# Attention, expert layer and a second layer in one kernel: float64 loads issued three jobs ahead, weight splits begun one step later

## The chip, the core and the metric

The kernel runs on one core of a Trainium2 chip. The core has a matrix engine (TensorE, PE in the rows), a vector engine (VectorE, DVE), a scalar engine (ScalarE, ACT), GpSimd (POOL) and SyncE (SP), which here only issues DMA transfers, all on one queue. Each engine takes its own instructions in order and waits for the others by semaphores. The metric is the device time of the whole program in microseconds, the median over several runs.

## The reference

```python
def _attn_ref(q, k, v, alpha):          # 2 batches, 8 heads, 768 tokens, 48 features, float32
    for t in range(S):
        state = alpha[:, :, t, :, None] * state + np.einsum('bhd,bhe->bhde', k[:, :, t], v[:, :, t])
        y[:, :, t] = np.einsum('bhd,bhde->bhe', q[:, :, t], state)

def _moe_ref(x, w_gate, w1, w2, capacity):      # 1536 tokens of 384, 8 experts of 1024, float32
    expert_idx = np.argmax(x @ w_gate, axis=1)  # each token goes to one expert, scaled by its gate
    h = np.maximum(np.einsum('ecd,edf->ecf', disp, w1), 0.0)
    y = np.einsum('ecf,efd->ecd', h, w2)

def _moe2_ref(x, w_in, w_out):          # 384 -> 2048 -> 384, both weights float64
    h = x @ w_in
    sp = np.where(h > 20.0, h, np.log1p(np.exp(np.minimum(h, 20.0))))
    return ((h * np.tanh(sp)) @ w_out).astype(np.float32)
```

## The kernel before

The program has three stages. In the **attention stage** (to about 80 us) the tokens go in 12 tiles of 128. Routing is part of it: each tile's rows are scattered by GpSimd (`scatter`, L108) into a table `tab` in DRAM, ordered by expert. Filler products (`keep_busy`, L783), whose results nobody reads, stand at the very start and in some gaps of TensorE.

The **expert stage** walks 8 experts with 8 steps each, 64 steps in all. At a step `g1` (L1052, nine matmuls) makes 128 hidden features for 240 tokens; ScalarE's ReLU writes `hh` (L1056) and VectorE the rest `hl` (L1057). `g2` (L1069, nine matmuls) of the step three before follows. Every product is made of three with operands split into a high and a low part. The result of `g1` goes to one of two PSUM banks in turn, so `g1` of step s waits until `hl` of step s−2 has been read out. Behind step 5 of an expert, `xpose` turns the next expert's tokens, gathered from `tab` (`gather`, L124), on TensorE.

The weights of w1 and w2 come in pieces of 128 x 768, two for each two steps: a DMA into a buffer `st` (L324; 8 buffers in `erl`, 6 in `wst`), the high part by ScalarE (`whi`, L336), the low part by VectorE (`wlo`, L342). `conv_to(n)` splits all pieces below n; `load_to` keeps the loads a fixed number of pieces ahead (`AHEAD`, 13). Step s calls `conv_to` with its bound behind its products.

Beside that the float64 weights `w_in` and `w_out` are made float32 in 17 jobs spread over steps 3 to 60 by the table `job_at`: `cvt_load` (L222, 512 KB into one of three buffers `big`), `cvt_a` (two ScalarE rows, L195 and L230, and two VectorE rows, L198 and L201) and `cvt_b` (one VectorE row, L206, and a store to DRAM, L238). Job 0 has its `cvt_a` at step 3 and its `cvt_b` at step 4, job 1 at 6 and 7, job 2 at 9 and 11, job 3 at 12 and 15, job 4 at 16 and 17. Behind `cvt_b(n)` the load of job n+2 is issued. The converted weights come back as pieces for the **last stage** (from 214 us), which is the second layer: `f1` (L1132), the activation, `f2` (L1175) and a scatter of the output rows.

Small works stand at fixed steps: `check_all` (whether the decay's inverse is good, L775 to L778) at step 0, `places` and `sort_places` at steps 1 and 2.

The order on every engine is that of the code (a manual schedule); waits follow from tiles that share a buffer. SP also waits with each transfer for the one issued eight before.

Of the kernel before, what the change touches and what calls it, by code (L numbers as in the profile page):

```python
# [23 lines left out]
def kernel(  # L24
# [41 lines left out]
    ATT = 4  # L66
# [4 lines left out]
    LEAD = 6  # L71
    WST = 6
# [11 lines left out]
    def w_new(i):  # L84
        p = wr_p[2 if i >= 76 else (i + 8) % 12 < 8]
        whi[i], wlo[i] = (p.tile([128, PW], F32R, tag=t, name=f"{t}{i}") for t in ("whi", "wlo"))
# [44 lines left out]
    bk = [ps.tile([128, 512], F32, name=f"bk{i}") for i in range(8)]  # L131
# [84 lines left out]
    def words(t):  # L216
        return t.bitcast(U32).rearrange("p (f two) -> p f two", two=2)

    def cvt_load(n):
        if n < len(cvt_jobs):  # L220
            t = words(fpool[0].tile([128, 2 * CN], F32, tag="big", name="w64", bufs=3)[:, 0:2 * cvt_jobs[n][1].shape[1]])
            nc.sync.dma_start(out=t, in_=words(cvt_jobs[n][0]))  # L222
            cvt_t[n] = [t]
# [35 lines left out]
    def late_load(n):  # L259
        if not 0 <= n < NLATE:  # L260
            return
        st = wst.tile([128, PW], F32, tag="st", name=f"sd{n}")
        fs = slice(FH + n // 2 * 128, FH + (n // 2 + 1) * 128)
        if n % 2:
            nc.sync.dma_start(out=words(st), in_=words(w_out[fs, :]))
        else:
            nc.sync.dma_start(
                out=st.bitcast(U32).rearrange("p (k f) -> p k f", k=KD),
                in_=w_in.bitcast(U32)[:, 2 * fs.start:2 * fs.stop].rearrange("(k p) f -> p k f", p=128),
            )  # L270
        late_t[n] = st
# [39 lines left out]
            hi, lo, w = late_t.pop(n)[3:]  # L311
            nc.vector.tensor_tensor(out=lo, in0=w, in1=hi.bitcast(F32), op=ALU.subtract)

    AHEAD = WST + 7
    conv_n, load_n, cvt_n = [0], [0], [0]

    def written(i):
        return min((i - E * NP1) // 4 * 6 + 6, len(cvt_jobs)) if i >= E * NP1 else 0

    def load_to(n):  # L320
        while load_n[0] < min(n, len(pieces)) and cvt_n[0] >= written(load_n[0]):
            i = load_n[0]
            st = raw_p[i % 14 >= 8].tile([128, PW], F32, tag="st", name=f"st{i}")
            nc.sync.dma_start(out=st.rearrange("p (a b) -> p a b", b=pieces[i].shape[2]), in_=pieces[i])  # L324
            wst_t[i] = st
            load_n[0] += 1
# [3 lines left out]
    def conv_high(n):  # L330
        while conv_n[0] < min(n, len(pieces)):
            i = conv_n[0]
            load_to(i + 1 + AHEAD)
            w = wst_t.pop(i)
            w_new(i)
            nc.scalar.activation(out=whi[i], in_=w, func=AF.Copy)  # L336
            low.append((i, w))
            conv_n[0] += 1

    def conv_low(n=None):  # L340
        for i, w in low[:n]:
            nc.vector.tensor_tensor(out=wlo[i], in0=w, in1=whi[i].bitcast(F32), op=ALU.subtract)  # L342
        del low[:n]

    def conv_to(n):
        conv_high(n)
        conv_low()
# [10 lines left out]
    with ExitStack() as actx:  # L358
# [414 lines left out]
        def check_all(cm):  # L773
            cmt = misc[0:1, 0:128]
            nc.tensor.transpose(out=cmt, in_=cm, identity=ident)  # L775
            cmx = const.tile([1, 1], F32, name="cmx")
            nc.vector.tensor_reduce(out=cmx, in_=cmt, axis=AX.X, op=ALU.min)
            nc.vector.tensor_scalar(out=bad, in0=cmx, scalar1=1.0, scalar2=None, op0=ALU.is_lt)  # L778


        def keep_busy(t, n):
            for _ in range(n):
                nc.tensor.matmul(out=t, lhsT=busy[:, 0:128], rhs=busy, start=True, stop=True)  # L783
# [56 lines left out]
                    )  # L840


        keep_busy(bk[6], 12)
        for h in range(2):
            load_an(0, range(h * HP // 2, (h + 1) * HP // 2))
        load(qn_t, 0, q_t, "qn")
# [138 lines left out]
        i = NTILE - 1  # L985
# [28 lines left out]
    x2l = x2p.tile([128, KD, XW], F32R, name="x2l")  # L1014
    fp = main.enter_context(tc.tile_pool(name="fp", bufs=2))
    fpool[0] = fp

    def big_tile():
        return fp.tile([128, 1024], F32, tag="big", name="big", bufs=3)
# [25 lines left out]
    def g1(e, m):  # L1045
        xh, xl = xt_e[e]
        wh, wl = w_first(e, m)
        hps = bk[2 + m % 2][:, m // 2 % 2 * WB:m // 2 % 2 * WB + WIN]
        n = 0
        for a, b_ in ((wh, xh), (wl, xh), (wh, xl)):  # L1050
            for kk in range(KD):
                nc.tensor.matmul(out=hps, lhsT=a[:, kk], rhs=b_[:, kk, :], start=(n == 0), stop=(n == 3 * KD - 1))  # L1052
                n += 1
        hh = fp.tile([128, WIN], F32R, tag="hh", name="hh", bufs=LAG + 1)
        hl = fp.tile([128, WIN], F32R, tag="hl", name="hl", bufs=LAG + 1)
        nc.scalar.activation(out=hh, in_=hps, func=AF.Relu)  # L1056
        nc.vector.scalar_tensor_tensor(  # L1057
            out=hl, in0=hps, scalar=0.0, in1=hh.bitcast(F32), op0=ALU.max, op1=ALU.subtract
        )
        h_t[e, m] = (hh, hl)  # L1060
# [27 lines left out]
    def y_out(e):  # L1088
        y_put(4 + e % 2 * 2, off_v.pop(e), free=e == E - 1)
# [4 lines left out]
    def place(col, engines=DYN):  # L1094
        return nc.values_load(meta_i[0:1, col:col + 1], engines=engines, min_val=0, max_val=NT)


    def places():
        nc.vector.tensor_tensor_scan(out=inc, data0=tot, data1=zn[:, 0:E], initial=0.0, op0=ALU.add, op1=ALU.add)
        nc.vector.tensor_tensor(out=off, in0=inc, in1=tot, op=ALU.subtract)  # L1100
        nc.vector.tensor_copy(out=meta_i, in_=off)


        nc.vector.scalar_tensor_tensor(
            out=slow_f, in0=mxc[0:1], scalar=float(WIN), in1=bad, op0=ALU.is_gt, op1=ALU.max
        )
# [113 lines left out]
    def at(n):  # L1220
        return steps[n] if 0 <= n < NS else None


    def f_mish(n):
        late = (n - EARLY) // 2 if n > EARLY else -9
        if n % 2 == 0:
            late_high(late - 1)
            sigma(at(n)) if at(n) else None
            late_size(late)
        elif at(n):  # L1230
            sigma(at(n))
        if n in last_of:
            bs = [at(i) for i in last_of[n]]
            cosine(bs)
        for m, c in full:
            (f_out if m >= MA else f_keep)(c)
        full.clear()
        now = list(due)
        due.clear()
        if n in last_of:  # L1240
            due.extend(bs)
        for b in now:
            gated(b)
        if n % 2:
            late_low(late - 2)
            late_join(late - 1)
            late_load(late + LATE_AHEAD - 1)
        conv_to(E * MF - EARLY + n + 3 + LEAD)

    def f_head(n):  # L1250
        if at(n):
            f1(at(n))
        f_mish(n)
# [28 lines left out]
        part(last, cs[3], True)  # L1282

    EARLY = LAG2
    CVT_END = 45
    LATE_AHEAD = 3
    xpose(0, False)
# [8 lines left out]
    for n in range(2 * len(cvt_jobs)):  # L1296
        job_at.setdefault(free[n * CVT_END // (2 * len(cvt_jobs))], []).append(((cvt_a, cvt_b)[n % 2], n // 2))
    for e in range(E):
        for m in range(MF):
            step = e * MF + m  # L1300
            if m == 6:
                off_v[e] = place(e)
            g1(e, m)
            pend.append((e, m))
            if len(pend) > LAG:
                pe, pm = pend.pop(0)
                g2(pe, pm)
                if pm == MF - 1:
                    y_out(pe)
            if e == E - 1 and m >= MF - EARLY:  # L1310
                f_head(m - MF + EARLY)
            conv_to(min(step + 1 + LEAD, ATT + (step + 1) * 9 // 8))
            if step == 0:
                cvt_load(0)
                cvt_load(1)
            for f, n in job_at.get(step, ()):
                f(n)
                if f is cvt_b:
                    cvt_load(n + 2)
            if step == 0:  # L1320
                check_all(cm)
            if step == 1:
                places()
            if step == 2:
                sort_places()
            if step % 4 == 3 and 0 < step // 4 <= NTILE:
                tok_scatter(step // 4 - 1)
            if e == E - 1 and m == 0:
                nc.sync.dma_start(
                    out=srt, in_=toks.rearrange("(c p) o -> p (c o)", p=128), allow_slow_non_contiguous=True  # L1330
                )
            if step == E * MF - 4:
                cvt_marks()
            if step == E * MF - 2:
                cvt_flag()
            if m == 5 and e + 1 < E:
                xpose(e + 1)
                if e + 2 < E:
                    gather(e + 2)
    for pe, pm in pend:  # L1340
        g2(pe, pm)
    apart.append(at(EARLY))
    f1(at(EARLY))
    y_out(E - 1)
# [240 lines left out]
```

## Time and profile before

| | |
|---|---|
| time, median of 3 runs | 433.04 us (432.83 to 433.56) |
| the profiled execution | 433.29 us, of it 431.0 us span from the first to the last instruction |
| TensorE busy | 413.6 us (96%) |
| VectorE busy | 325.6 us (76%) |
| ScalarE busy | 327.5 us (76%) |
| DMA | 68.89 MB, mean 160 GB/s |

Times in the rows below are counted from the start of the span. TensorE's busy time is modelled from pipelined matmuls, so idle time on it is the safer reading; the stages' limits differ, and the shares above are means over all of them.

### The profile page before, as it was taken

What the parts mean: (1) busy time and instruction counts of PE and PEld (TensorE: products, weight loads), DVE (VectorE), ACT (ScalarE), POOL (GpSimd) and SP (SyncE); (2) the same over time, 40 slices, a digit from 0 to 9 for tenths busy, and PEclk for the clock granted to TensorE, in tenths of its full rate; (3) what the DMA queues carried; (4) which work ended last, traced back from release to release, by engine and by line L of the source; (5) the groups of instructions that cost most, each with busy time, mean ns of one, the idle gap of its engine ahead of it and who ended that gap; (6) DMA issues with size and microseconds to landing.
All of it is one profiled execution on the core that took longest, in us unless ns stands there. A gap on an engine that the chain in (4) does not pass through costs nothing.

```text
span 431.0 us, 8400 instructions
## 1 busy us (share of the span) xinstructions
PE 413.6 (96%) x3122; PEld 376.7 (87%) x3126; DVE 325.6 (76%) x647; ACT 327.5 (76%) x579; POOL 61.4 (14%) x76
## 2 busy tenths in 40 slices
PE   7999989989999999999999999999999999999994
PEld 3887877789899999999988898989899898889893
DVE  7999997779799899988837875976697456475551
ACT  5887996668688787877779788878887877797630
POOL 5122666212011012000000000000000000003033
PEclk9899999999999999999999999999999999999999
DMA  7999996499999999995170112111000000001022
GB/s 226 331 299 320 321 364 236 149 318 247 364 334 328 321 287 314 297 337 189 40 238 0 39 36 74 38 37 53 23 1 2 0 2 0 2 1 73 2 75 78
DMA packets 51565, 68.89 MB, mean 160 GB/s; under 512 B 5500, under 2 KB 41852, under 8 KB 51516
## 3 DMA queue, kind: packets, MB, share of 16 engines
q1 hardware_dynamic: 49596, 63.55, 47.7%
q0 software_dynamic: 1920, 4.73, 3.0%
q8 instruction: 26, 0.43, 0.4%
q14 instruction: 23, 0.19, 0.2%
HBM read 56.65 MB, written 11.61 MB: 158 GB/s over the span
## 4 chain that ended last, share of the span: by engine, by line
PE 76%; DVE 9%; DMA 6%; ACT 4%; issue 2%; SPq 1%; POOL 0%; ACTq 0%; POOLq 0%; DVEq 0%
PE bk L1175 23%; PE bk L1132 22%; PE bk L1052 12%; PE bk L1069 11%; DMA w<-in_w_out_dram 2%; DVE pt L457 2%; PE bk L519 2%; DMA an<-in_alpha_t_dram 1%; DMA w<-in_w_in_dram 1%; PE bk L565 1%; DMA xs<-tab 1%; ACT whi L336 1%; PE bk L583 1%; PE bk L554 1%; PE bk L783 1%
## 5 line engine op out<-in xcount | busy, mean ns | idle before, releaser
L342 DVE TENSOR_TENSOR wlo<-st,whi 128x768 fp32r<-128x768 f32 x74 | 69.9, 951 | 16.1 <-ACT whi L336 15.2
L1160 DVE TENSOR_TENSOR p<-p,bk 128x512 f32<-128x512 f32 x48 | 32.8, 683 | 51.4 <-ACT p L1150 51.4
L1175 PE MATMUL bk<-whi,big 128*128 128x384 f32 x240 | 66.7, 338 | 0.8 <-DVE x2l L1079 0.8
L336 ACT ACTIVATE whi<-st 128x768 fp32r<-128x768 f32 x74 | 61.7, 842 | 0.0
L1144 ACT ACTIVATE p<-bk 128x512 f32<-128x512 f32 x48 | 28.8, 599 | 35.0 <-PE bk L1132 33.5
L1069 PE MATMUL bk<-hl,whi 128*128 128x240 f32 x192 | 52.8, 275 | 0.0
L1069 PE MATMUL bk<-hh,wlo 128*128 128x240 f32 x192 | 52.7, 274 | 0.0
L1069 PE MATMUL bk<-hh,whi 128*128 128x240 f32 x192 | 52.6, 274 | 0.0
L1175 PEld LDWEIGHTS bk<-whi,big 128*128 128x128 f32 x240 | 44.1, 188 | 2.6 <-DVE x2l L1079 1.1
L108 POOL DMA_INDIRECT out_dram<-acc,srt x12 | 12.2, 1018 | 233.9 <-DVE acc L1199 229.8
L1132 PE MATMUL bk<-x2l,whi 128*128 128x512 f32 x144 | 41.7, 397 | 0.0
L1132 PE MATMUL bk<-x2h,wlo 128*128 128x512 f32 x144 | 41.1, 394 | 0.0
L1132 PE MATMUL bk<-x2h,whi 128*128 128x512 f32 x144 | 41.0, 393 | 0.0
L1175 PE MATMUL bk<-wlo,big 128*128 128x384 f32 x120 | 40.6, 338 | 0.0
L1056 ACT ACTIVATE hh<-bk 128x240 fp32r<-128x240 f32 x64 | 23.5, 367 | 20.5 <-PE bk L1052 19.2
L1052 PE MATMUL bk<-xh,whi 128*128 128x240 f32 x192 | 33.6, 283 | 3.1 <-DVE hl L1057 2.7
L1069 PEld LDWEIGHTS bk<-hl,whi 128*128 128x128 f32 x192 | 36.3, 189 | 0.2 <-DVE hl L1057 0.2
L1069 PEld LDWEIGHTS bk<-hh,whi 128*128 128x128 f32 x192 | 36.4, 189 | 0.0
L1069 PEld LDWEIGHTS bk<-hh,wlo 128*128 128x128 f32 x192 | 36.3, 189 | 0.0
L1132 PEld LDWEIGHTS bk<-x2h,wlo 128*128 128x128 f32 x144 | 27.0, 188 | 6.7
L1132 PEld LDWEIGHTS bk<-x2l,whi 128*128 128x128 f32 x144 | 27.0, 188 | 6.3
L1150 ACT ACTIVATE p<-p,quarter 128x512 f32<-128x512 f32 x48 | 32.1, 717 | 0.3
(230 smaller groups left out, 967.2 us busy)
## 6 DMA issues: line engine op xcount, KB each, us to landing
st<-in_w_dram SPq DMA_DIRECT2D x64, 384.0 KB, 8.2
qn<-in_q_t_dram SPq DMA_DIRECT2D x12, 256.0 KB, 5.5
kn<-in_k_t_dram SPq DMA_DIRECT2D x12, 256.0 KB, 5.6
w<-in_w_in_dram SPq DMA_DIRECT2D x6, 512.0 KB, 6.2
w<-in_w_out_dram SPq DMA_DIRECT2D x6, 512.0 KB, 7.7
tab<-zero SPq DMA_DIRECT2D x4, 720.0 KB, 7.1
an<-in_alpha_t_dram SPq DMA_DIRECT2D x11, 256.0 KB, 6.0
vn<-in_v_n_dram SPq DMA_DIRECT2D x12, 192.0 KB, 4.5
```

The source lines that it names most:

```text
L108: r = nc.gpsimd.indirect_dma_start(out=dst[:, :], out_offset=bass.IndirectOffsetOnAxis(ap=idx, axis=0), in_=src, in_offset=None, bounds_ch ...
L336: nc.scalar.activation(out=whi[i], in_=w, func=AF.Copy)
L342: nc.vector.tensor_tensor(out=wlo[i], in0=w, in1=whi[i].bitcast(F32), op=ALU.subtract)
L457: nc.vector.tensor_tensor_scan(out=pt[0:R2, c], data0=at[0:R2, c], data1=starts[0:R2, c], initial=0.0, op0=ALU.mult, op1=ALU.add)
L1052: nc.tensor.matmul(out=hps, lhsT=a[:, kk], rhs=b_[:, kk, :], start=(n == 0), stop=(n == 3 * KD - 1))
L1056: nc.scalar.activation(out=hh, in_=hps, func=AF.Relu)
L1069: nc.tensor.matmul(out=y[n], lhsT=a[:, ns], rhs=b_, start=(m == 0 and t == 0 and n % 2 == 0), stop=(m == MF - 1 and t == 2), skip_group_ch ...
L1132: r = nc.tensor.matmul(out=hps, lhsT=a[:, kk], rhs=b_[:, kk, w0:w0 + wd], start=(n == 0), stop=(n == 3 * KD - 1))
L1144: nc.scalar.activation(out=p, in_=h2_t[b], func=AF.Sigmoid, scale=-1.0)
L1150: nc.scalar.activation(out=p_t[b], in_=p_t[b], func=AF.Sin, scale=-2.0, bias=quarter)
L1160: nc.vector.tensor_tensor(out=g, in0=g, in1=h2_t.pop(b), op=ALU.mult)
L1175: nc.tensor.matmul(out=o_t[c], lhsT=a[:, ts], rhs=b_, start=(m in (0, MA) and n == 0), stop=(m in (MA - 1, MF2 - 1) and n == 2),)
```

## The change

Four things move. The float64 loads of jobs 0, 1 and 2 are issued ahead of the first `xpose`, directly behind the attention stage, and each `cvt_b(n)` is followed by the load of job n+3 instead of n+2. The loads of weight pieces run 10 ahead until then (`ahead`), 13 afterwards, so that pieces 14 to 16 are no longer loaded at the end of the attention stage. Step s splits the pieces below 4 + 9s/8 instead of 4 + 9(s+1)/8, as far as the other bound (s + 7) doesn't come first: none at step 0, and the same count as before from step 24. The check and the flag that it feeds (now a function of its own, `slow_at`) move from steps 0 and 1 to step 3. And the first filler has 14 products instead of 12.

```diff
-    AHEAD = WST + 7
+    ahead = [WST + 4]
...
-            load_to(i + 1 + AHEAD)
+            load_to(i + 1 + ahead[0])
...
-        keep_busy(bk[6], 12)
+        keep_busy(bk[6], 14)
...
     fpool[0] = fp
+    ahead[0] = WST + 7
...
         nc.vector.tensor_copy(out=meta_i, in_=off)
 
-
+    def slow_at():
         nc.vector.scalar_tensor_tensor(
             out=slow_f, in0=mxc[0:1], scalar=float(WIN), in1=bad, op0=ALU.is_gt, op1=ALU.max
         )
...
     EARLY = LAG2
+    for n in range(3):
+        cvt_load(n)
     CVT_END = 45
...
-            conv_to(min(step + 1 + LEAD, ATT + (step + 1) * 9 // 8))
-            if step == 0:
-                cvt_load(0)
-                cvt_load(1)
+            conv_to(min(step + 1 + LEAD, ATT + step * 9 // 8))
             for f, n in job_at.get(step, ()):
                 f(n)
                 if f is cvt_b:
-                    cvt_load(n + 2)
-            if step == 0:
+                    cvt_load(n + 3)
+            if step == 3:
                 check_all(cm)
+                slow_at()
```

On SP, before, from the first gather (`xs`) of the expert stage on; `st` is a weight piece (14 is the first of them), `w` a float64 load:

```order
L124 DMA xs<-tab 128x384
L124 DMA xs<-tab 112x384
L324 DMA st_1338<-in_w_dram 128x3x256
L324 DMA st_1343<-in_w_dram 128x2x384
L324 DMA st_1348<-in_w_dram 128x3x256
L124 DMA xs<-tab 128x384
L124 DMA xs<-tab 112x384
L324 DMA st_1408<-in_w_dram 128x2x384
L222 DMA w_1414<-in_w_in_dram 128x1024
L222 DMA w_1416<-in_w_in_dram 128x1024
L324 DMA st_1435<-in_w_dram 128x3x256
```

The same place now, with the semaphores that each transfer waits for (DVE, Activation, Pool, PE: an engine's; DMAHW: an earlier transfer of SP's; DMASW: a scatter of GpSimd's has landed):

```order
L124 DMA xs_1300<-tab_77 112x384 [waits DMAHW6_49]
L222 DMA w64_1377<-in_w_in_dram 128x1024 [waits DVE_49,DMAHW7_49,Activation_49,Pool_49]
L222 DMA w64_1379<-in_w_in_dram 128x1024 [waits DMAHW0_49]
L222 DMA w64_1381<-in_w_in_dram 128x1024 [waits DMAHW1_49]
L124 DMA xs_1394<-tab_77 128x384 [waits DMAHW2_49,DMAHW5_49,DMASW3_49,DMAHW6_49,DMASW2_49,PE_49]
L124 DMA xs_1394<-tab_77 112x384 [waits DMAHW3_49]
L324 DMA st14_1423<-in_w1_dram 128x3x256 [waits DMAHW4_49,DVE_49]
L324 DMA st15_1425<-in_w2_dram 128x2x384 [waits DVE_49]
L324 DMA st16_1427<-in_w1_dram 128x3x256 [waits DVE_49]
L324 DMA st17_1429<-in_w2_dram 128x2x384 [waits DMAHW7_49,DVE_49,Activation_49]
```

The three float64 loads stand ahead of the second gather, and pieces 14 to 16 have gone from ahead of it to behind it.

On VectorE, before, from the low part of piece 3 to `hl` of step 2:

```order
L342 TENSOR_TENSOR wlo_1351<-st_888,whi_1350 128x768
L1057 SCALAR_TENSOR_TENSOR hl<-bk_88,hh 128x240
L342 TENSOR_TENSOR wlo_1411<-st_890,whi_1410 128x768
L777 TENSOR_REDUCE cmx<-bk_93 1x1
L778 TENSOR_SCALAR bad<-cmx 1x1
L1057 SCALAR_TENSOR_TENSOR hl<-bk_89,hh 128x240
L342 TENSOR_TENSOR wlo_1438<-st_997,whi_1437 128x768
L1099 SCALAR_TENSOR_TENSOR inc<-bk_93,zn 128x8
L1100 TENSOR_TENSOR off<-inc,bk_93 128x8
L1101 CAST meta_i<-off 128x8
L1104 SCALAR_TENSOR_TENSOR slow_f<-mxc,bad 1x1
L1057 SCALAR_TENSOR_TENSOR hl<-bk_88,hh 128x240
```

And now, from the same low part to `hl` of step 2:

```order
L342 TENSOR_TENSOR wlo_1347<-st_890,whi_1346 128x768
L1058 SCALAR_TENSOR_TENSOR hl<-bk_88,hh 128x240
L1058 SCALAR_TENSOR_TENSOR hl<-bk_89,hh 128x240
L342 TENSOR_TENSOR wlo_1432<-st_892,whi_1431 128x768
L1100 SCALAR_TENSOR_TENSOR inc<-bk_93,zn 128x8
L1101 TENSOR_TENSOR off<-inc,bk_93 128x8
L1102 CAST meta_i<-off 128x8
L1058 SCALAR_TENSOR_TENSOR hl<-bk_88,hh 128x240
```

The two `hl` of steps 0 and 1 follow each other; one low part stands between `hl` of steps 1 and 2, and the check's rows (`cmx`, `bad`) and the flag's (`slow_f`) are gone from here.

## Rows read from the trace of the kernel before

**Rows 1.** Stages: length, busy time of each engine (instructions), granted clock, DMA share, GB/s.

```profile
83.30:120.70 37.40, 34.65 (x292) 33.37 (x293) 32.42 (x64) 27.18 (x55) 4.92 (x4) 1.00 1.00 312
120.70:214.70 94.00, 94.00 (x843) 94.00 (x842) 86.51 (x154) 72.88 (x152) 9.27 (x8) 1.00 0.91 273
214.70:423.00 208.30, 207.49 (x1065) 187.39 (x1064) 133.03 (x242) 163.50 (x227) 10.24 (x10) 1.00 0.12 37
```

**Rows 2.** Waits, 78 to 125 us: who waited for whom, us, times, longest.

```profile
ACT wm L195 <- DMA w<-in_w_in_dram: 3.1, 1, 3.1
...
PE bk L1052 <- DVE hl L1057: 2.7, 5, 0.8
```

**Rows 3.** TensorE's timeline, 78 to 125 us: start, duration, instruction, idle before.

```profile
83.33 0.64 PE L1052 MATMUL bk<-xh,whi 128*128 128x240 f32 x3 [0.38 <-ACT xh L1041]
...
87.64 0.60 PE L1052 MATMUL bk<-xh,whi 128*128 128x240 f32 x3 [0.75 <-DVE hl L1057]
...
95.42 0.60 PE L1052 MATMUL bk<-xh,whi 128*128 128x240 f32 x3 [0.84 <-DVE hl L1057]
...
112.75 0.78 PE L1024 MATMUL bk<-ident,xs 128*128 128x128 f32 x6
...
118.59 0.60 PE L1052 MATMUL bk<-xh,whi 128*128 128x240 f32 x3 [0.20 <-DVE hl L1057]
```

**Rows 4.** The chain that ended last, 60 to 126 us: start, us, what.

```profile
87.23 5.89 DMA w<-in_w_in_dram
...
104.64 9.16 DMA w<-in_w_out_dram
...
122.89 1.01 PE bk L1052 x9
123.90 1.00 PE bk L1069 x9
```

**Rows 5.** SP's queue, timeline: the second gather.

```profile
85.88 0.82 SPq L124 DMA_DIRECT2D xs<-tab  x2
```

**Rows 6.** VectorE's timeline, 78 to 125 us.

```profile
85.95 0.96 DVE L342 TENSOR_TENSOR wlo<-st,whi 128x768 fp32r<-128x768 f32 x1 [0.38 <-ACT whi L336]
86.82 0.27 DVE L777 TENSOR_REDUCE cmx<-bk 1x1 f32<-1x128 f32 x1
...
87.20 0.39 DVE L1057 SCALAR_TENSOR_TENSOR hl<-bk,hh 128x240 fp32r<-128x240 f32 x1
...
93.60 0.69 DVE L201 SCALAR_TENSOR_TENSOR wt<-w,wt 128x512 uint32<-128x512 uint32 x1
```

**Rows 7.** ScalarE's timeline, 78 to 130 us.

```profile
79.94 0.58 ACT L743 ACTIVATE xg_l<-bk,gt 128x384 f32<-128x384 f32 x1 [0.48 <-DVE jr L749]
...
85.07 0.84 ACT L336 ACTIVATE whi<-st 128x768 fp32r<-128x768 f32 x1
85.87 0.37 ACT L1056 ACTIVATE hh<-bk 128x240 fp32r<-128x240 f32 x1
...
93.14 0.68 ACT L195 ACTIVATE wm<-w 128x512 f32<-128x512 f32 x1 [3.08 <-DMA w<-in_w_in_dram]
```

**Rows 8.** Tile `w` (the float64 loads), 80 to 215 us: issue to landing.

```profile
DMA to landing us min/median/max: 5.7/7.1/9.2
```

**Rows 9.** Tile `xs` (the gathers), 74 to 125 us: issue to landing.

```profile
DMA to landing us min/median/max: 2.6/4.7/8.8
```

**Rows 10.** TensorE's timeline, 0 to 24 us.

```profile
1.27 5.30 PE L783 MATMUL bk<-busy 128*128 128x512 bf16 x12 [1.27 <-DVE busy L138]
7.28 0.71 PE L519 MATMUL bk<-q,kp 48*128 48x128 f32 x8 [0.71 <-DVE kp L811]
...
14.51 1.16 PE L519 MATMUL bk<-q,kp 48*128 48x128 f32 x16 [0.73 <-DVE kp L502]
```

**Rows 11.** Half-microsecond windows, as rows 1: first and last of six with that clock.

```profile
10.00:10.50 0.50, 0.50 (x2) 0.00 (x0) 0.29 (x1) 0.50 (x2) 0.50 (x1) 0.50 0.96 281
...
12.50:13.00 0.50, 0.50 (x11) 0.50 (x9) 0.50 (x1) 0.48 (x1) 0.00 (x0) 0.50 1.04 383
```

## The prediction

> **What bounds the kernel now.** I read the stages first, then the waits, then the chain that ended last, then each engine's timeline where that chain leaves TensorE. The stages [rows 1]: from 214.7 us to 423 TensorE is busy 207.49 of 208.30 us, and from 120.7 to 214.7 all of 94.00. Whatever makes TensorE reach the place it has at 120.7 earlier moves the end by as much. Between 83.3 and 120.7 it is busy 34.65 of 37.40 us. There it waits 2.7 us in five waits for VectorE's `hl`, and ScalarE waits 3.1 us once for a float64 load [rows 2].
>
> The chain says why [rows 4]: a float64 load issued at 87.23 lands after 5.89 us, and one issued at 104.64 after 9.16. Each holds up ScalarE and VectorE, which take their instructions in order, so the ReLU rows `hh` and `hl` queued behind the job are late, and TensorE's first product two steps on waits for them: step 6 at 95.42 after 0.84 us idle, step 16 at 118.59 still with 0.20 [rows 3]. One wait has no load in it: at 87.64 step 3 waits 0.75 us, since VectorE does piece 4's low part (85.95) and the check (86.82) before `hl` of step 1 (87.20) [rows 6].
>
> How much is there to win before 120.7? A first product costs 1.01 us, a second 1.00 [rows 4], a set of transposes at most 0.78 [rows 3]. Step 16 begins after 16 first products, 13 second ones and two sets: 16.2 + 13.0 + 1.6 = 30.8 us, so at 114.1 counted from 83.33, against 118.59. The ceiling is 4.5 us: 2.7 idle, the rest slow restarts (three matmuls behind a wait take 0.60 us) and waits too short for the list.
>
> **Term 1, splits one step on, check at step 3.** Behind `hl` of step 0 VectorE now does `hl` of step 1 at once. ScalarE's `hh` of step 1 (0.37 us) no longer stands behind piece 4's high part (0.84) [rows 7]. So `hl` of step 1 ends at about 86.4, before the third first product does (86.8), and step 3 starts at 86.8 instead of 87.64: 0.8 us. What is late next: piece 4's low part, now done at about 87.9; step 4 needs it at 88.9, so 1 us of cover is left there. Without it, each microsecond costs one. Up to step 24 as many as two pieces fewer are split by any step, 1.9 us of VectorE (0.96 each, [rows 6]); they are caught up where TensorE is the bound. The check itself, one TensorE row and three short VectorE rows, only moves.
>
> **Term 2, loads three ahead, three of them early.** Before, jobs 0 and 1 are issued from 87.23 on, behind three weight pieces and a gather (85.88) [rows 4, 5]. Now three loads stand directly behind the first gather. The first waits for VectorE, ScalarE and GpSimd, and for no scatter's landing; the ScalarE one I resolve to the row at 79.94, which ends at 80.52 [rows 7]. So they go out at 80.6 to 81.5. A float64 load lands after 5.7 to 9.2 us [rows 8]: job 0 between 86.3 and 89.8. ScalarE comes to it at about 89.1, behind `hh` of step 3, and would wait 0 to 0.7 us; I take 0, since until 85.9 only the last scatters share the DMA. Jobs 1 and 2 are used steps later. Job 3 is issued after job 0's store (about 95.2 instead of 104.64), lands by 104.4 at the longest, and is needed at about 107. Each later load likewise gets three steps (6 us) more, by the order of the jobs. Three buffers suffice: the load that takes one again stands behind its last reader.
>
> Moved behind the three on SP: gather 1, which goes out no earlier than its scatter allows (85.88 before, and again), and pieces 14 to 17, some 5 us later than before, at 87 to 88. ScalarE wants piece 14 at step 10, about 102; that is the cover, and if it were gone each microsecond late would stop ScalarE by one.
>
> **The walk.** I took the three engines through the changed order with the durations of [rows 3, 4, 6, 7], each instruction beginning when its engine is free and what it reads is there. Done over the old order, with the landings of [rows 4], this gives 118.6 for step 16, where the row has 118.59. For the new order: step 3 at 86.8, step 6 at 93.5 (job 0's two splits end at 92.5, the check costs 0.5, `hl` of step 4 ends at 93.4), step 16 at 114.6, with one wait of 0.35 us left and four under 0.15. Three restarts at 0.1 us each make it 114.9. The gain is 118.6 − 114.9 = 3.7 us.
>
> **Term 3, two more filler products.** Twelve take 5.30 us from 1.27; the first real product starts at 7.28 after 0.71 us idle [rows 10]. Two more end at about 7.4: the scores' first half may move by 0.1 us, their second half waits for VectorE anyway, so 0. From 10.0 to 13.0 us the granted clock is 0.50 [rows 11], so 1.2 GHz, after a start with idle time in it. If the fuller start keeps 2.4 GHz, TensorE ends that work earlier, but at 14.51 it waits 0.73 us for VectorE's `kp` [rows 10]: again 0. If the fall only comes later, in the dense stretch behind 14.5, 3 us at half speed cost up to 1.5. The Trainium skill ("TensorE: Matmul & The Clock Gate", Part 1) has the throttled state as the default, released by activity; by that the fuller start would help or do nothing, and the sum stays.
>
> **Sum.** The profiled execution took 433.29 us (span 431.0 and 2.3 around it): 433.29 − 3.7 = 429.6. The median of the runs lies 0.25 below it, so 429.3.
>
> **Rivals.**
> - *The gather comes late.* Its transposes are due at 92.9 in the walk. From 85.9, the usual 4.7 us bring it in at 90.6, the longest, 8.8, at 94.7 [rows 9]: 1.8 us of waiting. With the 0.7 us of job 0 the gain falls to between 1.2 and 3: 430.0 to 431.8. For it: the DMA's share is 1.00 up to 120.7 [rows 1]. Against: in the same traffic gather 1 was in time. The Trainium skill ("DMA: Bandwidth & Descriptors", Queues, rings and completion order) speaks for it: an engine takes one ring's descriptors in order, so the gather waits for all of the 1.57 MB ahead. By that rule, at 312 GB/s [rows 1] from about 82.5 on, 1.6 us of it are left at 85.9, and the gather lands at 92.2: the sum would stay, by 0.7 us.
> - *The DMA is the bound.* If the 11.7 MB of 83.3 to 120.7 (37.4 us at 312 GB/s) can't go faster, TensorE waits for pieces instead, and the time stays within 0.2% of 433.0 (0.9 us, about what a measurement of this kernel can tell from no change). Against: no piece's landing is in the chain there, and behind 120.7 the rate falls to 273 GB/s, so the queue is not full for good [rows 1].
> - *Slower.* The load at SP's head waits longer than I resolved, for the last scatter (85.7), through a shared buffer. The three then go out from 85.8, the gather at 87.2 with 5.0 us of traffic ahead of its own 4.7: 96.9. Step 6 begins at 97.5 instead of 95.42, 2.1 us lost; of the later waits 1.1 us (2.7 − 0.75 − 0.84) are still saved: 434.0. It decides once the gather lands after 95.9. Against: the order names no scatter among that load's waits.
> - *A moved clock fall* (term 3) alone leaves 430.8.
>
> **How the numbers follow.** Forecast 0.66 (own range 428.5, the ceiling, to 430.0); late gather or moved fall 0.20; DMA bound 0.08; slower 0.06. So faster 0.86, same 0.08, slower 0.06. The range 428.4 to 431.6 leaves out the last two and little else.
>
> **What would show it.** Right: float64 loads issued at 80.6 to 81.5; no ScalarE wait for one before 125 us; step 3 at about 86.8, step 6 at 93.5, step 16 at 114.6 to 115; TensorE without a gap from there. Wrong: transposes that wait for `xs` near 93, ScalarE waiting for pieces 14 to 17 near 102, a low part late at step 4, or the three loads starting after 85.

## The result, and the profile after

The changed kernel takes 428.58 us (median of four runs, 428.08 to 429.61), against 432.94 us for the kernel before beside it: a ratio of 0.9892, 95% interval 0.9862 to 0.9922. The forecast was 429.3 us, a ratio of 0.9914. The side holds; the time of the changed kernel lies 0.7 us under the forecast, and the gain of this comparison lies just beyond the low end of the range (0.9892 of the 433.04 us shown before is 428.36; the range began at 428.4). Ratios, here and below, leave out the single executions more than 1.5% above the fastest of their kernel, and they are not exactly the quotients of the medians.

The profiled execution took 428.67 us, of it 426.5 us span. Its stages, columns as in [rows 1]:

```profile
83.30:116.00 32.70, 32.70 (x292) 32.55 (x291) 31.37 (x64) 25.97 (x52) 5.43 (x4) 1.00 0.94 298
116.00:210.00 94.00, 94.00 (x842) 93.84 (x841) 86.76 (x154) 74.23 (x154) 9.40 (x8) 1.00 0.93 288
210.00:418.00 208.00, 207.19 (x1064) 187.14 (x1063) 132.99 (x242) 163.43 (x227) 9.97 (x10) 1.00 0.12 37
```

The same 292 matrix products that filled 34.65 of 37.40 us now fill 32.70 of 32.70: TensorE has no gap left before 116 us, and none was opened behind it. The waits from 78 to 125 us (who waited for whom, us, times, longest) have turned round: ScalarE waits for TensorE, and neither wait of [rows 2] is there. A third wait of before, which [rows 2] leaves out, is gone too: ScalarE's second one for a float64 load in that window, for job 3 at 113.82. The first line is that wait before, the second the longest of ScalarE and TensorE now.

```profile
ACT wm L195 <- DMA w<-in_w_out_dram: 2.8, 1, 2.8
...
ACT hh L1057 <- PE bk L1053: 7.2, 11, 1.2
```

TensorE's timeline, the products of steps 0, 3, 6 and 16 and the first transposes, as in [rows 3]:

```profile
82.78 0.64 PE L1053 MATMUL bk<-xh,whi 128*128 128x240 f32 x3 [0.38 <-ACT xh L1042]
...
86.18 0.50 PE L1053 MATMUL bk<-xh,whi 128*128 128x240 f32 x3
...
92.36 0.78 PE L1025 MATMUL bk<-ident,xs 128*128 128x128 f32 x6
...
92.91 0.58 PE L1053 MATMUL bk<-xh,whi 128*128 128x240 f32 x3
...
113.86 0.50 PE L1053 MATMUL bk<-xh,whi 128*128 128x240 f32 x3
```

Step 16 begins 31.08 us behind step 0, where it was 118.59 − 83.33 = 35.26 us: 4.18 us of the gain. And step 0 itself begins at 82.78 instead of 83.33: 0.55 us, from a stage that the prediction took as fixed. Of the 4.73 us at step 16, 4.5 reach the end of the span. VectorE's scan that set the 14.51 of [rows 10] shows where the 0.55 comes from; before, it began at 11.20 us after a wait of 0.91 us for the same transfer, `an`:

```profile
10.65 1.23 DVE L457 TENSOR_TENSOR_SCAN pt<-an,bk 112x516 f32<-112x516 f32 x1 [0.49 <-DMA an<-in_alpha_t_dram]
```

From there on both kernels keep step: VectorE's first `kp` row behind that scan begins at 13.77 us before and at 13.23 after, the last of the stage at 69.76 and 69.20. So in these two executions the half microsecond is the landing of one transfer. That landing falls in the six windows of [rows 11], whose clock is now 1.00 throughout; here is the first:

```profile
10.00:10.50 0.50, 0.34 (x2) 0.00 (x0) 0.17 (x1) 0.50 (x2) 0.50 (x1) 1.00 1.09 353
```

On SP the three early loads go out at 80.03, the second gather 2.1 us later than in [rows 5], and the pieces behind it at 88.88:

```profile
80.03 1.46 SPq L222 DMA_DIRECT2D w<-in_w_in_dram  x3
87.98 0.80 SPq L124 DMA_DIRECT2D xs<-tab  x2
88.88 5.22 SPq L324 DMA_DIRECT2D st<-in_w_dram  x7
```

### The profile page after: what moved, and what is told of

The parts are those of the page before. It is cut to its first block, busy times and chain, and to the rows that moved or that the text cites. A ratio compares the mean times of both kernels' runs of the same rounds, so it can differ in the third digit from the quotient of the medians.

```text
span 426.5 us, 8419 instructions
## 1 busy us (share of the span) xinstructions
PE 411.2 (96%) x3124; PEld 375.6 (88%) x3128; DVE 325.1 (76%) x647; ACT 327.6 (77%) x579; POOL 62.2 (15%) x76
## 3 DMA queue, kind: packets, MB, share of 16 engines
q0 software_dynamic: 1920, 4.73, 3.0%
## 4 chain that ended last, share of the span: by engine, by line
PE 82%; DVE 10%; ACT 2%; issue 2%; DMA 1%; SPq 1%; POOL 0%; POOLq 0%; DVEq 0%
PE bk L1176 23%; PE bk L1133 23%; PE bk L1053 15%; PE bk L1070 14%; DVE pt L457 2%; PE bk L519 2%; DMA an<-in_alpha_t_dram 1%; DVE kp L502 1%; PE bk L1025 1%; PE bk L565 1%; DVE s L602 1%; PE bk L583 1%; DVE q L506 1%; DVE er L484 1%; PE bk L783 1%
```

## The experiments

All kernels of one comparison ran on one chip, beside the kernel before. Five comparisons followed, with five rounds each.

| kernel | median us | before beside it | ratio (95%) |
|---|---|---|---|
| e_fill14 | 432.14 | 431.89 | 1.0017 (0.9987 to 1.0047) |
| e_fill12 | 428.62 | 431.89 | 0.9920 (0.9902 to 0.9938) |
| e_loads | 429.26 | 431.89 | 0.9931 (0.9914 to 0.9947) |
| e_splits | 431.35 | 431.89 | 0.9987 (0.9964 to 1.0011) |
| e_again (the changed kernel) | 428.67 | 431.78 | 0.9941 (0.9915 to 0.9966) |
| e_two | 431.22 | 431.78 | 0.9992 (0.9972 to 1.0013) |
| e_behind | 428.69 | 431.78 | 0.9936 (0.9913 to 0.9959) |
| e_bound | 429.10 | 431.78 | 0.9936 (0.9920 to 0.9952) |
| e_check0 | 429.50 | 432.92 | 0.9923 (0.9909 to 0.9937) |
| e_dma2 | 442.72 | 432.92 | 1.0231 (1.0196 to 1.0266) |
| e_gather2 | 431.42 | 432.92 | 0.9976 (0.9958 to 0.9994) |
| e_an2 | 429.32 | 432.92 | 0.9910 (0.9894 to 0.9926) |
| e_before2 (the kernel before) | 433.00 | 432.88 | 0.9999 (0.9983 to 1.0015) |
| e_again2 (the changed kernel) | 430.02 | 432.88 | 0.9922 (0.9896 to 0.9948) |
| e_an2b | 429.52 | 432.88 | 0.9914 (0.9889 to 0.9939) |
| e_fill4 | 429.91 | 432.88 | 0.9927 (0.9901 to 0.9952) |
| e_behind2 | 428.59 | 431.69 | 0.9922 (0.9892 to 0.9952) |
| e_again3 (the changed kernel) | 428.60 | 431.69 | 0.9918 (0.9889 to 0.9947) |

The fourth and fifth comparison (from e_check0 and from e_before2 on) are about 1 us longer throughout: there VectorE's last two `kp` rows of the attention stage begin 9.2 us apart in every profile, elsewhere 8.25, with a pause of several engines near 65 us that the profile puts to no instruction. So kernels are compared within a comparison.

From TensorE's timeline of each profile: where step 0 begins, and steps 3, 6 and 16 counted from it (us).

| kernel | step 0 | step 3 | step 6 | step 16 |
|---|---|---|---|---|
| before; e_fill14; e_before2 | 83.33; 82.59; 84.58 | 4.31; 4.31; 4.31 | 12.09; 12.00; 11.85 | 35.26; 34.05; 33.83 |
| after; e_again; e_again3; e_fill12 | 82.78; 82.72; 83.06; 83.02 | 3.40 to 3.41 | 10.13 to 10.15 | 31.08; 31.10; 31.08; 31.08 |
| e_loads | 82.36 | 4.31 | 11.01 | 31.87 |
| e_splits | 82.32 | 3.40 | 11.27 | 32.71 |
| e_two | 82.47 | 3.40 | 10.14 | 31.70 |
| e_behind; e_behind2 | 83.01; 82.83 | 3.42; 3.40 | 10.74; 10.14 | 32.17; 31.09 |
| e_bound | 82.95 | 3.95 | 10.77 | 31.81 |
| e_check0 | 83.55 | 3.40 | 10.26 | 31.12 |
| e_again2 | 83.88 | 3.40 | 10.41 | 31.89 |
| e_an2; e_an2b; e_fill4 | 83.44; 83.94; 84.42 | 3.40 | 10.15; 10.13; 10.14 | 31.08; 31.08; 31.08 |

**The filler alone, and the change without it.**

```diff
-        keep_busy(bk[6], 12)
+        keep_busy(bk[6], 14)
```

> The kernel before with 14 filler products in place of 12 and nothing else. The prediction (term 3 worth 0): within 0.1 us of before, expert stage's first product at 83.3. Rival A, the filler is worth the 0.55 us that the changed kernel already has at the scores of tile 1 (13.97 against 14.51): about 0.5 us faster than before, granted clock 1.00 from 10 to 13 us, first product of the expert stage near 82.8. Rival B, the 0.55 us is a difference from one execution to the next (the landing of a decay transfer): time equal to before, and the scores of tile 1 at either 14.0 or 14.5 whatever the clock.

> The changed kernel with the 12 filler products of before. The prediction: equal to the changed kernel (428.6, about 4.4 us under before), whether the clock falls at 10 us or not. Rival A: about 0.5 us slower than the changed kernel (429.1), granted clock 0.50 from 10 to 13 us and tile 1's scores at 14.5. Rival B: equal in time to the changed kernel, with tile 1's scores at either place.

Neither moves the time. In e_fill12 the clock fell between 8.5 and 12 us, and its ratio to before (0.9920) lies among the changed kernel's four (0.9892 to 0.9941); in e_fill14 it did not, and it is no faster than before. Term 3's zero holds.

**One half of the change each.** e_loads is the kernel before with only these lines of the change:

```diff
+    ahead = [WST + 4]
...
+    ahead[0] = WST + 7
...
+    for n in range(3):
+        cvt_load(n)
...
+                    cvt_load(n + 3)
```

e_splits is the kernel before with the rest, but for the filler:

```diff
+            conv_to(min(step + 1 + LEAD, ATT + step * 9 // 8))
...
+            if step == 3:
                 check_all(cm)
+                slow_at()
```

> The kernel before with only the float64 loads moved (three at once behind the attention stage, three jobs ahead, weight pieces 10 ahead until then). By the walk of the prediction step 3 stays at 87.8, step 6 comes at 94.4 and step 16 at 115.3 instead of 118.6: 3.3 us faster than before, and no wait of ScalarE for a float64 load. If instead the gather or the DMA takes most of it back: 1 to 2 us faster.

> The kernel before with only the splits one step on and the check at step 3. By the walk step 3 comes 0.8 us sooner, at 86.8, but ScalarE then waits about 4.0 instead of 3.1 us for the float64 load of job 0, step 6 stays at 95.4 and step 16 at 118.6: no change in time (0.0 us). If the 0.8 us of term 1 counts by itself: 0.8 us faster.

e_loads takes 0.6 us more than e_fill12 on the same chip, which the two intervals don't tell from nothing; its stage is 0.79 us longer at step 16. e_splits is within the measurement of before. TensorE of e_splits, from 84 to 180 us:

```profile
85.72 0.50 PE L1052 MATMUL bk<-xh,whi 128*128 128x240 f32 x3
...
93.59 0.61 PE L1052 MATMUL bk<-xh,whi 128*128 128x240 f32 x3 [0.90 <-DVE hl L1057]
...
158.76 0.61 PE L1052 MATMUL bk<-xh,whi 128*128 128x240 f32 x3 [2.00 <-DVE hl L1057]
```

Of the 0.9 us won at step 3, 0.6 to 0.8 are left at step 6, although ScalarE then waits 3.3 us for job 0, and step 16 comes 1.1 to 2.5 us sooner than in the three profiles with the old stage. It is lost later. The last row, step 36, is new: a load issued at 145.80 lands after 10.67 us and stops ScalarE at a job that cost the profiled execution of before nothing. At step 63 e_splits is 137.36 us behind its step 0, the three others 135.90 to 137.46. The expected 0.0 us came, but not by the expected way.

```profile
156.49 0.67 ACT L195 ACTIVATE wm<-w 128x512 f32<-128x512 f32 x1 [3.62 <-DMA w<-in_w_out_dram]
```

**Early without three ahead, three ahead without early.**

```diff
-    for n in range(3):
+    for n in range(2):
         cvt_load(n)
...
-                    cvt_load(n + 3)
+                    cvt_load(n + 2)
```

```diff
-    for n in range(3):
-        cvt_load(n)
...
     gather(1)
+    for n in range(3):
+        cvt_load(n)
```

> The changed kernel unaltered, beside the three kernels below and for a second profile of it. If the stage from step 0 to step 16 has no wait left that depends on a transfer, its 31.08 us come back within 0.05 us. Where the stage begins (82.78 us before) comes from the attention stage: by rival B of the filler runs it differs from one execution to the next by some tenths, up or down.

> The changed kernel with two float64 loads ahead of the passage in place of three, and each later load two jobs ahead as before: the early issue without the longer distance. If the gain is that of the early issue: equal to the changed kernel within 0.2 us, since job 3's load then goes out at about 96 and lands by 106 at the longest, when ScalarE comes to it. If the distance of three is what frees the later jobs: waits of ScalarE for a float64 load at step 12 or later, 0.5 to 1.5 us slower than the changed kernel.

> The changed kernel with its three first float64 loads issued behind the second gather instead of ahead of it: the distance of three without the early issue. By the walk ScalarE waits about 4 us for job 0 (landing near 92.5), step 6 comes 2.0 us later than in the changed kernel and step 16 2.4 us later: 2.0 to 2.4 us slower than the changed kernel, and the second gather goes out near 85.5. If the early issue were worth nothing because the gather is late behind it: equal or faster.

> The changed kernel with its three first loads behind the second gather, again. If the early issue counts: a wait of ScalarE for job 0's load of 2.5 us or more, step 16 some 32.2 us behind step 0 and the median about 1 us over the changed kernel's beside it. If the wait is given back somewhere: equal medians again, within 0.3 us.

> The changed kernel unaltered, beside the one above: step 16 at 31.1 us behind step 0, 428.6 to 430.0 us by the chip.

This is the surprise. With the distance of two, early or not, the time is that of before: 2.5 us over the changed kernel on the same chip. The expectation of "equal" rested on job 3's load going out at about 96; SP got to it at 100.73. Two of ScalarE's six waits for float64 loads in e_two:

```profile
102.06 0.68 ACT L195 ACTIVATE wm<-w 128x512 f32<-128x512 f32 x1 [1.00 <-DMA w<-in_w_in_dram]
109.40 0.68 ACT L195 ACTIVATE wm<-w 128x512 f32<-128x512 f32 x1 [2.12 <-DMA w<-in_w_out_dram]
```

The loads behind them were issued by SP at

```profile
94.38 0.43 SPq L222 DMA_DIRECT2D w<-in_w_in_dram  x1
100.73 0.43 SPq L222 DMA_DIRECT2D w<-in_w_out_dram  x1
```

so they took 7.7 and 8.7 us, where ScalarE came to them after 6.7 and 6.6 (102.06 − 1.00 − 94.38, and 109.40 − 2.12 − 100.73). In this profile (430.40 us, one of e_two's shorter executions) TensorE waits for `hl` at steps 16 and 36; it is 0.6 us behind e_again at step 16 and 2.1 us at step 63 (135.26 against 133.17 us from step 0). As in e_splits, part of what is won early is lost to a later load. With the loads behind the second gather, on the other hand, the time is the changed kernel's in both comparisons. In e_behind's profile ScalarE waited 2.7 us for job 0 and step 16 came 1.1 us later; in e_behind2's it waited

```profile
89.37 0.67 ACT L195 ACTIVATE wm<-w 128x512 f32<-128x512 f32 x1 [0.83 <-DMA w<-in_w_in_dram]
```

and step 6 was not late at all. Behind the gather the loads go out at 84.5 to 84.9, not at 87.23 as before: pieces 14 to 16 no longer stand ahead of the gather on SP, and the gather itself goes out near 84 instead of at 85.88. So the loads' place ahead of the gather is worth nothing that the medians show, and a microsecond in an execution in which job 0 lands late.

**The bound and the check apart.**

```diff
-            conv_to(min(step + 1 + LEAD, ATT + step * 9 // 8))
+            conv_to(min(step + 1 + LEAD, ATT + (step + 1) * 9 // 8))
```

> The changed kernel with the old bound of the splits (one step earlier), the check left at step 3. By the walk step 3 comes some 0.4 us later, since piece 4's low part stands ahead of hl of step 1 again and only the check is gone: 0.4 us slower than the changed kernel at step 16. If the check was the whole of term 1: equal to the changed kernel.

In e_check0 the bound stays as changed:

```diff
-            if step == 3:
+            if step == 0:
                 check_all(cm)
                 slow_at()
```

> The changed kernel with the check and its flag put back to step 0, the splits one step on as in the change. Between hl of step 0 and hl of step 1 VectorE then has only the check's rows (0.4 us). If the two halves of term 1 add up (the bound 0.55 at step 3, the check 0.36, as the two kernels with the old bound give by difference): step 3 at 3.4 to 3.8 us behind step 0 and step 16 within 0.4 us of the changed kernel's 31.08, so 0 to 0.4 us slower. If the check alone is what held hl of step 1: 0.8 us slower.

By the profiles the bound is nearly the whole of term 1: 0.55 us at step 3 and 0.7 at step 16 without it. The medians, 0.4 us apart, can't show it (0.9936 and 0.9941, with overlapping intervals). By e_check0's profile (step 16 at 31.12 us; its median has no changed kernel beside it) the check costs nothing at step 0 once no piece's low part stands beside it; it showed (4.31 − 3.95 = 0.36 us at step 3) only in company.

**The DMA, and the gather.** e_dma2 copies each load's data (512 KB for nine of them, 256 or 384 KB for the last five) once more, from job 3 on, to an unused place in DRAM.

```diff
             nc.sync.dma_start(out=t, in_=words(cvt_jobs[n][0]))
+            if n >= 3:
+                nc.sync.dma_start(out=words(scr[n, :, 0:2 * cvt_jobs[n][1].shape[1]]), in_=words(cvt_jobs[n][0]))
```

In e_gather2 the second gather moves into the loop:

```diff
-    gather(1)
...
+            if step == 1:
+                gather(1)
             for f, n in job_at.get(step, ()):
```

> The changed kernel, and behind each float64 load from job 3 on a copy of the same 512 KB from DRAM to an unused place in DRAM: 14 copies, 7 MB more read and 7 MB more written while steps 4 to 60 run, nothing else. If the DMA's rate were what bounds the expert stage (the rival), each copy would cost its 0.5 MB at about 300 GB/s, 1.7 us or more, 20 us in all. If the queue has room there and the distance of three jobs covers it: landings of the float64 loads some us later, but no wait of ScalarE for one and less than 0.5 us slower.

> The changed kernel with the second gather issued at step 1, behind weight pieces 14 to 17, in place of ahead of them. The gather then no longer holds the pieces back (they go out near 82), but it goes out some microseconds later itself, near 90 or later. If the rival's condition is right that the transposes at 92.4 have nothing to spare (they waited 0.2 us for the gather in the changed kernel), each microsecond of its later landing costs one: 1 to 4 us slower, with a wait for xs ahead of step 6. If it has room: equal.

Neither expectation of e_dma2 is met: it costs 13 us over e_check0's 429.5 on the same chip, less than 20 and far more than 0.5. What gives way first is not the float64 loads but the gathers, which lie in the same queue and have no distance. TensorE in e_dma2, and the sums from 78 to 215 us:

```profile
148.77 1.36 PE L1028 MATMUL bk<-ident,xs 128*128 128x128 f32 x6 [3.79 <-DMA xs<-tab]
...
172.35 0.55 PE L1028 MATMUL bk<-ident,xs 128*128 128x128 f32 x3 [4.40 <-DMA xs<-tab]
```

```profile
PE bk L1028 <- DMA xs<-tab: 9.2, 4, 4.4
ACT wm L196 <- DMA w<-in_w_out_dram: 1.6, 1, 1.6
```

So the 13 us are not a price that each copy pays. In this profiled execution the first and the last set of transposes in that window lie 116.09 us apart, in e_check0 100.52: of the 15.6 us more, 9.2 are these waits. Most of the rest is TensorE's clock, which was granted at 0.50 (1.2 GHz) for some 3 us behind the wait of 3.79 us and some 6 us behind that of 4.40; by an estimate, half of those 9 us is lost. The second stretch, columns as in [rows 1]:

```profile
173.00:179.00 6.00, 5.64 (x27) 5.64 (x28) 3.06 (x6) 3.31 (x7) 0.98 (x1) 0.50 1.04 377
```

e_gather2 takes about 2 us more than e_check0 beside it. Its profiled execution took 438.30 us, 6.9 over its median, so only that the wait exists is read from it: the transposes ahead of step 6 waited 1.82 us for `xs`. The rival's condition, a gather late at step 6, is thus real, and it has little to spare: in e_again2, the changed kernel on another chip, the first transposes take 1.04 instead of 0.78 us and the second ones 1.11, with their second part late by the gather, step 16 comes at 31.89, and a later gather holds TensorE outright.

```profile
162.44 0.84 PE L1025 MATMUL bk<-ident,xs 128*128 128x128 f32 x6 [0.76 <-DMA xs<-tab]
```

**The start.** What sets where step 0 begins?

> The changed kernel with the third decay transfer of the start issued two places earlier, ahead of the first value tile and the second key tile. In four profiles VectorE waits 0.17 to 0.91 us at about 10.5 us for that transfer and in two it does not, and the expert stage begins at 82.3 to 83.3. If that landing is what moves the start of the stage from execution to execution: no wait there, first product of the expert stage near 82.3, 0.3 to 0.5 us faster than the changed kernel. If VectorE is held by something else right behind it: equal.

> The changed kernel with the third decay transfer two places earlier, again, now beside the changed kernel itself. If that landing sets the start: no wait of VectorE at 10 us, kp of tile 1 at 12.8 instead of 13.0 to 13.4, and 0.2 to 0.6 us faster than the changed kernel. If the gain is lost later: equal.

> The kernel before unaltered, for a second profile of it. If the start is set by the landing of one decay transfer, VectorE's first kp of tile 1 lies anywhere between 12.8 and 13.8 us (13.77 in the first profile) and the expert stage begins 69.5 us behind it whatever the place. In the stage, from step 0 to step 16, 34 to 35.3 us, by how late the float64 loads of jobs 0 and 3 land. If the 13.77 belongs to the kernel: 13.7 to 13.8 again.

> The changed kernel unaltered, beside the others on this chip. Stage of 31.1 us again, start by the landing as in the two profiles before; 428.6 us, or up to 1 us more where the chip pauses in the attention stage, as the kernels of the last comparison did at 65 us.

> The changed kernel with 4 filler products in place of 14, so about 4 us of idle TensorE at the start. Term 3 of the prediction: the clock falls to 0.50 in some stretch, and it costs nothing as long as TensorE waits for VectorE's kp at 13 to 14.5 us behind it: equal to the changed kernel. If the filler is what keeps the start short: kp of tile 1 later than 13.5 us or a low clock behind 14 us, 0.5 to 1.5 us slower.

```diff
+        load_an(2)
         load(vn_t, 0, v_n, "vn")
         load(kn_t, 1, k_t, "kn")
-        load_an(2)
```

That is the edit of e_an2 and e_an2b; e_before2 and e_again2 are the two kernels unaltered, and e_fill4 has

```diff
-        keep_busy(bk[6], 14)
+        keep_busy(bk[6], 4)
```

The earlier transfer takes its wait away in both profiles (the scan begins at 9.96 and 10.11 us), but so it did in e_again2 with the old order (10.13), and the interval of e_an2b overlaps that of e_again2: equal as far as it can be told. e_before2 shows the late landing again, so the "anywhere" of its expectation is not shown for before itself:

```profile
11.12 1.23 DVE L457 TENSOR_TENSOR_SCAN pt<-an,bk 112x516 f32<-112x516 f32 x1 [0.97 <-DMA an<-in_alpha_t_dram]
```

But e_loads and e_splits, with the same start, had the first `kp` at 12.79 and 12.77, a microsecond sooner. What it is worth in the time these runs don't show: one profile gives one landing, and the medians don't follow it (`kp` at 13.44 with 4 filler products and at 12.96 in e_again2; medians 429.91 and 430.02).

## Why the prediction was right, and where it was wrong

- **What bounds the kernel**: shown. With the float64 waits gone the stage has no idle time, and the end follows.
- **Term 1 (0.8 us)**: right in size. e_loads is 31.87 − 31.08 = 0.79 us longer at step 16. Without the loads moved it shows nothing in the median (e_splits): in that profile it was ahead at step 16 and lost it to one late load at step 36. The check's part in it was wrong: nearly all of it is the bound.
- **Term 2**: right in effect, wrong in its reason. The loads went out at 80.0 (forecast 80.6, less the 0.55 of the start), ScalarE came to job 0 at 88.4 and waited for none. But most of the gain is the distance of three jobs: 2.5 of 3.1 us on one chip (e_two against e_again). The place ahead of the gather, which the text describes first, is worth 0 in the median (e_behind, e_behind2). Behind the gather the loads still go out sooner than before, 1.6 to 1.9 us behind step 0 instead of 3.3 to 3.9; what that part is worth no run separates. "ScalarE waits 3.1 us once" misses its second wait, 2.8 us for job 3, which lies in the same window.
- **"Gather 1 goes out no earlier than its scatter allows (85.88 before, and again)"**: wrong, 87.98. The last scatter itself landed later, with 1.57 MB of loads issued beside it; SP waited 6.3 us for it instead of 2.0. The transposes at 92.36 were still on time. From the scatter's issue to that of the gather behind it there are 3.1 and 3.3 us with no load beside it (e_behind2, e_behind), 4.6 to 4.9 with pieces 14 to 16 (before, e_before2, e_fill14, e_splits), 5.5 with two float64 loads (e_two) and 6.9 to 7.9 with three (the changed kernel): so the float64 loads beside the scatter make it land later. The Trainium skill ("DMA: Bandwidth & Descriptors", Queues, rings and completion order) made the gather late by way of its own ring; here the gather was late before it was issued, and 4.4 us behind its issue the transposes ran. The same section of the Trainium skill also says that an engine takes turns between the queues that have work for it, and that is the part which bears on a scatter of GpSimd's own queue landing later.
- **Pieces 14 to 17 "at 87 to 88"**: seven pieces from 88.88 to 94.1, hidden as forecast.
- **Term 3 (0)**: right, by e_fill14, e_fill12 and e_fill4.
- **The step that failed is the walk's remainder, and with it the 3.7 us of the sum**: "one wait of 0.35 us left and four under 0.15. Three restarts at 0.1 us each make it 114.9", 31.57 us from step 0 to step 16. Of the four profiles of the changed kernel three give 31.08 to 31.10 (the fourth, e_again2, had late gathers), and e_fill12, e_an2, e_an2b and e_fill4 31.08, so the stage gave 35.26 − 31.08 = 4.18 us. In the first profile no wait is listed there, and one such restart is left, at step 2 (the row at 85.07 takes 0.60 us). The difference of 31.57 and 31.08 is 0.5 of the 0.7 us by which the forecast missed. The recorded text doesn't place the wait; a likely place is step 9, whose `hl` of step 7 stands behind job 1's rows: in the trace it begins at 98.49, takes 0.40 us, and step 9 begins at 99.04 without a wait.
- **The rest is the base.** Start (0.55 us) and stage (35.26 us) of before were taken from one execution, and a change of the start was put at nothing. Two more profiles with that stage's code have 34.05 and 33.83 us: how much the loads cost depends on how late they land. The low end of the range came from a ceiling of 4.5 us, counted from that execution, with the start held fixed and 0.78 us for a set of transposes, which holds TensorE for only 0.55 (92.36 to 92.91). The measured gain, 0.55 + 4.18 us at step 16, lies beyond it by the start, not by the stage. The error has no fixed sign: the changed kernel's ratio is 0.9892, 0.9941, 0.9922 and 0.9918 in four comparisons, around the 0.9914 of the forecast; three of the four lie within the range, so the side of it on which the first fell is in part luck. What stays open is why the four runs of before in the first comparison lie 1 us over those of the second, third and sixth; only one of them has a profile.
- **Rivals**: "DMA is the bound" and "slower" did not come. "Late gather" did not come in the first profile, came with some 0.8 us at step 16 in e_again2, and in e_dma2 it is what gives way first.

## What to carry to other kernels

A transfer that lands after 4 to 10 us (4.3 to 10.2 for the float64 loads of the changed kernel's first profile) needs a distance that covers the longest landing, counted from when its queue really gets to it: here two jobs (6.6 us) lost to some load in every profile, three lost to one load (1.2 us, in e_again2) in all profiles of the changed kernel, and whether the first ones stood ahead of the gather or behind it didn't matter to the median. A gain that removes waits for transfers differs from execution to execution by as much as the waits do, so its base is several profiles, not one. And when loads are moved ahead, look at what shares the queue without a distance of its own: here, with more traffic, the gathers are what failed first.

## What the runs showed of the hardware

The recorded clock and the products' durations can disagree. In e_fill4 the granted clock reads 1.00 from 8 to 13 us, yet TensorE's rows up to about 12 us are those of the low clock; the scores at 6.62 take 1.23 us for eight products, where the changed kernel takes 0.72:

```profile
1.27 1.89 PE L783 MATMUL bk<-busy 128*128 128x512 bf16 x4 [1.27 <-DVE busy L138]
6.62 1.23 PE L519 MATMUL bk<-q,kp 48*128 48x128 f32 x8 [3.46 <-DVE kp L811]
...
10.36 1.49 PE L783 MATMUL bk<-busy 128*128 128x512 bf16 x3
```

The first four filler products take 0.47 us each in a stretch recorded as 1.00, and the three at 10.36 take 0.50 each; in the changed kernel three at 9.53 take 0.81 together, in e_fill12, where the recorded clock is 0.50, three at 10.46 take 1.48. So the engine began at the slow level (1.2 GHz), and with a start of 4 products and 3.46 us idle behind them it stayed there. The Trainium skill ("TensorE: Matmul & The Clock Gate", Part 1) says both, that the throttled state is the default and that the clock's trace events are not to be trusted alone; the rows agree. With 12 filler products the recorded clock fell to 0.50 near 9 to 13 us in three of five profiles (before, e_before2, e_fill12), with 14 in none of fourteen, and the time did not follow in either case. In the expert stage it did: e_dma2's clock fell behind 3.79 and 4.40 us without a product.
